# A small store of zeros ahead of ScalarE's loads, in a kernel that scales an image by channel

## The chip, the cores and the metric

The kernel runs on one core of a Trainium2 chip. The metric is the device time of one execution in microseconds (us). Before the change the median of the three runs was 530.68 us (530.67 to 531.29).

## The reference

```python
# x: [1, 384, 384, 384] bf16 (113.25 MB), w1d: [1] bf16
g = einsum("bhwc->bc", x) / (H * W)      # mean of each channel
s = sigmoid(g * w1d[0])                  # k = 1: one weight
return x * s[:, None, None, :]           # another 113.25 MB
```

The input must be read once and the output written once, 226.5 MB together. A strict reading needs the mean of all of x before the first element can be written. The kernel gets round this: it computes a scale `s_early` from the first tile alone, multiplies everything with it, sums up the whole of x on TensorE along the way, computes the true scale `s_true` at the end, and repeats the work only if the two differ after rounding to bf16. They don't with this input.

## The kernel before: the parts that matter

The image is cut into 27 tiles, 25 of them of 128 partitions x 44 rows x 384 channels (4.33 MB) and two smaller ones at the end. Six of them fit into SBUF at once. The first four are loaded in halves, one half from SyncE's queue and one from ScalarE's; all further loads come from SyncE and all stores from ScalarE.

```python
def load(place, n, r0, queues=("sync",)):
    ...
    for queue, m in zip(queues, split(n, -(-n // len(queues)))):
        plan.dma(queue, at(place + i, m), of[:, i * C : (i + m) * C],
                 writes=rows(place + i, m))
        i += m

def put(place, n, r0, to):
    plan.op("vector", gate(to, place, n, s_early), ...)      # x * s_early
    plan.final.append(
        plan.dma("scalar", dram(o_rows, r0, n), at(to, n), reads=rows(to, n)))

# cut: add_rows (TensorE sums a tile), add_banks, weight
plan.op("vector", lambda e: e.memset(ones[:], 1.0), writes=["ones"])
for k in range(BOTH):                                        # BOTH = 4
    load(places[k], sizes[k], starts[k], ("sync", "scalar"))
    if k == 0:
        plan.dma("scalar", w_one[0:1, 0:1], w1d.unsqueeze(0), writes=["w_one"])
weight()
add_rows(places[0], sizes[0], 0, True, True)
add_banks(0, copy=True)
# cut: s_early = sigmoid(total * w), on ScalarE
for k in range(1, len(sizes)):
    if k >= n_slots:                                         # n_slots = 6
        j = k - n_slots
        put(places[j], sizes[j], starts[j], places[j])       # store tile k - 6
    if k >= BOTH:
        load(places[k], sizes[k], starts[k])                 # waits for that store
    add_rows(places[k], sizes[k], 1, k == 1, k == last)
# cut: the last stores, s_true, the comparison, the second pass
```

Of the kernel before, what the change touches and what calls it, by code (L numbers as in the profile page):

```python
# [3 lines left out]
P = 128  # L4
ROW = 384
BF16 = mybir.dt.bfloat16
# [99 lines left out]
def split(n, most):  # L106
    k = -(-n // most)
    return [n // k + (i < n % k) for i in range(k)]
# [6 lines left out]
def bass_standalone__channel_attn_eca__vision_kernel(  # L115
# [5 lines left out]
    B, H, W, C = x.shape  # L121
    assert B == 1 and C == ROW and (B * H * W) % (4 * P) == 0
    n_rows = B * H * W // P
    x_rows, o_rows = x.flatten_outer_dims(), out.flatten_outer_dims()

    def dram(view, r0, n):
        return view[r0 * P : (r0 + n) * P, :].rearrange("(p t) c -> p (t c)", p=P)
# [3 lines left out]
    s_true = nc.alloc_sbuf_tensor("s_true", [P, C], BF16)  # L131
    w_one = nc.alloc_sbuf_tensor("w_one", [1, 16], BF16)
    w_scaled = nc.alloc_sbuf_tensor("w_scaled", [P, 2], F32)
    warm = nc.alloc_sbuf_tensor("warm", [P, 2], F32)
    wrong = nc.alloc_sbuf_tensor("wrong", [P, 1], F32)
    redo = nc.alloc_sbuf_tensor("redo", [P, 1], I32)
# [9 lines left out]
    def at(r0, n):  # L146
        assert r0 + n <= n_arena
        return arena[:, r0 * C : (r0 + n) * C]

    def rows(r0, n):  # L150
        return [("sb", r) for r in range(r0, r0 + n)]

    def gate(to, place, n, s):
        s_b = s[:].unsqueeze(1).broadcast_to([P, n, C])
        v, to_v = (at(r, n).rearrange("p (t c) -> p t c", t=n) for r in (place, to))
        return lambda e: e.tensor_tensor(to_v, v, s_b, ALU.mult)  # L156
# [5 lines left out]
    sizes = [EDGE] + [SLOT] * full + [4 * q for q in split(rest // 4, EDGE // 4)]  # L162
    assert sum(sizes) == n_rows and max(sizes) <= SLOT
    plan = Planner(nc, "a", 50)
# [51 lines left out]
    def add_banks(group, copy):  # L216

        for m, lo, hi in ((0, 0, C), (0, C, WIDE), (1, 0, 256), (1, 256, WIDE),
# [9 lines left out]
                )  # L228
            plan.op("vector", emit, reads=[f"acc{group}", "total"], writes=["total"])

    def put(place, n, r0, to):
        plan.op(
            "vector",
            gate(to, place, n, s_early),
            reads=["s_early"] + rows(place, n),
            writes=rows(to, n),
        )
        plan.final.append(
            plan.dma("scalar", dram(o_rows, r0, n), at(to, n), reads=rows(to, n))
        )  # L240

    def weight():
# [28 lines left out]


    plan.op("gpsimd", lambda e: e.memset(warm[:, 0:1], 0.0), writes=["warm"])  # L273
    plan.op("vector", lambda e: e.memset(ones[:], 1.0), writes=["ones"])  # L274
    for k in range(BOTH):
        load(places[k], sizes[k], starts[k], ("sync", "scalar"))
# [10 lines left out]
        reads=["total", "w_scaled0", "warm1"],  # L287
        writes=["s_early"],
# [4 lines left out]
    for k in range(1, len(sizes)):  # L293
        if k >= n_slots:
            j = k - n_slots
            put(places[j], sizes[j], starts[j], places[j])
        if k >= BOTH:
            load(places[k], sizes[k], starts[k])
        add_rows(places[k], sizes[k], 1, k == 1, k == last)
    for k in range(len(sizes) - n_slots, last):  # L300
        put(places[k], sizes[k], starts[k], places[k])
    put(places[last], sizes[last], starts[last], places[last + 1 - n_slots])


# [6 lines left out]
        reads=["total", "w_scaled1"],  # L311
        writes=["s_true"],
# [6 lines left out]
        reads=["s_true", "s_early"],  # L319
        writes=["total"],  # L320
# [4 lines left out]
        reads=["total"],  # L325
        writes=["wrong"],
# [4 lines left out]
        reads=["wrong"],  # L331
        writes=["redo"],
# [5 lines left out]
    for place, n, r0 in zip(places, sizes, starts):  # L338
# [4 lines left out]
            reads=rows(place, n),  # L343
            writes=rows(place, n),
# [74 lines left out]
```

## Time and profile before

| | before |
|---|---|
| time, median of 3 runs | 530.68 us |
| span in the profile | 528.7 us |
| TensorE and VectorE busy | 46% each |
| DMA, mean over the span | 429 GB/s |

These lines are from the page of the kernel before. "DMA" is the busy share of the core's 16 DMA engines in tenths, in 40 equal slices of the span; "GB/s" is what they moved in each slice. The last two lines are DMA issues: the queue that issues them (ACTq is ScalarE's, SPq SyncE's), the KB of each and the median time in us from issue to landing.

```profile
span 528.7 us, 1091 instructions
...
DMA  8999999999999999999999999999999999999998
GB/s 359 431 427 419 447 429 431 445 414 447 419 442 437 422 447 412 450 428 430 440 419 450 430 429 435 424 450 430 430 431 427 447 429 430 429 443 433 430 420 349
...
HBM read 113.25 MB, written 113.25 MB: 428 GB/s over the span
...
out_dram<-arena ACTq DMA_DIRECT2D x25, 4224.0 KB, 62.3
arena<-in_x_dram SPq DMA_DIRECT2D x21, 4224.0 KB, 38.7
```

The DMA engines are full from the second slice to the last but one, and no compute engine comes close. The windows say the same with numbers (a packet is counted whole in the window in which it starts, so a share can pass 1). Columns: the window in us from the start of the span, its length, busy time of each engine with the count of instructions, TensorE's granted clock, the share of the DMA engines' time, and GB/s in the last column. Kernel before:

```profile
core 0: us, PE busy (x) PEld busy (x) DVE busy (x) ACT busy (x) POOL busy (x), PEclk, DMA share, GB/s
0.00:5.00 5.00, 0.00 (x0) 0.00 (x0) 0.17 (x1) 1.49 (x2) 0.30 (x5) 1.00 0.68 237
...
35.00:60.00 25.00, 15.57 (x65) 0.00 (x0) 24.28 (x4) 0.00 (x0) 0.00 (x0) 0.91 1.02 433
60.00:110.00 50.00, 24.77 (x79) 0.00 (x0) 20.86 (x3) 0.00 (x0) 0.00 (x0) 0.64 1.00 432
110.00:500.00 390.00, 184.59 (x646) 0.00 (x0) 179.61 (x21) 0.00 (x0) 0.00 (x0) 0.73 1.00 433
```

The next lines are from the timeline of the beginning, kernel before: start in us, duration in us, engine, line, operation, tiles; what stands in brackets at the end is the idle time just ahead and what ended it. A DMA's duration here is the time its queue took to issue it, not the transfer.

```profile
0.73 0.41 ACTq L91 DMA_DIRECT2D arena<-in_x_dram  x1
...
0.74 2.96 SPq L91 DMA_DIRECT2D arena<-in_x_dram  x6
...
1.17 0.54 ACTq L91 DMA_DIRECT2D w_one<-in_w1d_dram  x1
1.74 1.59 ACTq L91 DMA_DIRECT2D arena<-in_x_dram  x3
...
14.13 0.16 PE L252 MATMUL w_all<-w_one,ones 1*128 1x1 bf16 x1 [14.13 <-DMA w_one<-in_w1d_dram]
...
25.92 0.61 ACT L284 ACTIVATE s_early<-total,w_scaled 128x384 bf16<-128x384 f32 x1 [21.06 <-DVE total L226]
...
35.56 18.07 ACTq L91 DMA_DIRECT2D out_dram<-arena  x3
```

By 3.7 us, SyncE has issued six loads and ScalarE four. TensorE's first matmul waits for the weight, which stands in ScalarE's queue behind a half tile and is there at 14.1 us. `s_early` is made at 25.9 us and the first store is issued at 35.6 us. From then on the kernel has one rhythm, which the chain of waits shows (start, duration, what; "another core or an unknown queue" here is the time of a DMA that the profile doesn't name). Kernel before:

```profile
44.43 41.95 DMA out_dram<-arena
...
86.45 0.33 SPq L91
86.78 19.55 another core or an unknown queue
...
106.39 0.33 SPq L91
```

SyncE issues a load every 19.9 us, each time when a store has landed and freed its place. A tile loaded and a tile stored are 8.65 MB, and 8.65 MB in 19.9 us is about 433 GB/s again: the rhythm is set by the DMA engines' rate.

The trace also has a record of every DMA packet; the packet figures in this document are worked out from these records, and none of the views printed here shows them. Here one packet is one partition's piece, 16,896 bytes for a half tile and 33,792 for a whole one. A large piece takes 1.251 us on its engine, and 16 engines at that pace make 432.2 GB/s. "Lost", below, is the time by which the DMAs are behind that rate. In the kernel before they lose 2.56 us first (the first packet starts only at 1.75 us, and the first ones are slow), about 0.4 us around 44 us, where the first store begins, and 2.2 us at the end, where the engines don't finish together and the last packet ends at 527.8 us, 0.9 us before the span does.

### The profile page before, as it was taken

Reading aid. Unit: us, or ns where it says so; the run is one execution under the profiler, and the core shown is the slowest. Engines: PE = TensorE matmul, PEld = TensorE weight load, DVE = VectorE, ACT = ScalarE, POOL = GpSimd, SP = SyncE. Lnnn points to the kernel's source line nnn. Section 1 sums busy time; section 2 is a strip of 40 time slices with the busy share of each in tenths; the row PEclk is TensorE's granted clock in tenths of the full one; section 3 lists DMA queues with packets and bytes.
Section 4 is the critical chain, followed back from the end, with each engine's and each line's share of the span. In section 5 each row is a group of like instructions: output and inputs, shape, how many; then the busy total and the mean of one; then the engine's idle time right before and its main releaser. Section 6 shows DMA issues by size and latency. Waiting matters only on the chain.

```text
span 528.7 us, 1091 instructions
## 1 busy us (share of the span) xinstructions
PE 245.2 (46%) x865; PEld 0.2 (0%) x2; DVE 241.2 (46%) x45; ACT 2.7 (1%) x4; POOL 0.3 (0%) x5
## 2 busy tenths in 40 slices
PE   0877256165275165174274364264373373365400
PEld 0000000000000000000000000000000000000000
DVE  0299742633624633624624624624615615616720
ACT  1000000000000000000000000000000000000000
POOL 0000000000000000000000000000000000000000
PEclk9989776686676786786875786886875776877665
DMA  8999999999999999999999999999999999999998
GB/s 359 431 427 419 447 429 431 445 414 447 419 442 437 422 447 412 450 428 430 440 419 450 430 429 435 424 450 430 430 431 427 447 429 430 429 443 433 430 420 349
DMA packets 8360, 226.57 MB, mean 429 GB/s; under 512 B 930, under 2 KB 930, under 8 KB 930
## 3 DMA queue, kind: packets, MB, share of 16 engines
q10 hardware_dynamic: 4466, 121.90, 53.5%
q1 hardware_dynamic: 3888, 104.60, 46.1%
q8 instruction: 3, 0.05, 0.0%
q14 instruction: 3, 0.02, 0.0%
HBM read 113.25 MB, written 113.25 MB: 428 GB/s over the span
## 4 chain that ended last, share of the span: by engine, by line
another core or an unknown queue 70%; DMA 16%; DVE 4%; PE 3%; SPq 1%; issue 1%; ACT 0%; ACTq 0%
DMA out_dram<-arena 8%; DMA arena<-in_x_dram 6%; PE acc L184 3%; DVE arena L156 3%; DMA w_one<-in_w1d_dram 2%; SPq L91 1%; DVE total L226 1%; ACT s_true L308 0%; ACT s_early L284 0%; DVE total L316 0%; DVE total L224 0%; DVE wrong L324 0%; PE acc L182 0%; ACTq L91 0%
## 5 line engine op out<-in xcount | busy, mean ns | idle before, releaser
L184 PE MATMUL acc<-arena,ones 128*128 128x512 bf16 x863 | 244.7, 454 | 244.0 <-DMA arena<-in_x_dram 244.0
L156 DVE TENSOR_TENSOR arena<-arena,s_early 128x16896 bf16<-128x16896 bf16 (+2 forms) x27 | 234.5, 8691 | 240.9 <-PE acc L184 237.5
L252 PE MATMUL w_all<-w_one,ones 1*128 1x1 bf16 x1 | 0.2, 159 | 14.1 <-DMA w_one<-in_w1d_dram 14.1
L261 DVE TENSOR_SCALAR w_scaled<-w_all 128x1 f32<-128x1 f32 x2 | 0.2, 152 | 13.3 <-PE w_all L252 13.3
L226 DVE TENSOR_TENSOR total<-total,acc 128x128 f32<-128x128 f32 (+2 forms) x11 | 4.5, 408 | 2.4 <-PE acc L184 2.0
L224 DVE COPY total<-acc 128x384 f32<-128x384 f32 x1 | 0.6, 558 | 8.6 <-PE acc L184 8.6
L308 ACT ACTIVATE s_true<-total,w_scaled 128x384 bf16<-128x384 f32 x1 | 0.6, 614 | 479.5 <-DVE total L226 479.5
L246 ACT ACT_TABLE_LOAD x1 | 1.3, 1283 | 3.4 <-issue 3.4
L316 DVE TENSOR_TENSOR total<-s_true,s_early 128x384 f32<-128x384 uint16 x1 | 0.6, 559 | 0.7 <-ACT s_true L308 0.7
L284 ACT ACTIVATE s_early<-total,w_scaled 128x384 bf16<-128x384 f32 x1 | 0.6, 614 | 21.1 <-DVE total L226 21.1
L182 PE MATMUL acc<-arena,ones 128*128 128x512 bf16 x1 | 0.6, 590 | 0.0
L324 DVE TENSOR_REDUCE wrong<-total 128x1 f32<-128x384 f32 x1 | 0.6, 553 | 0.0
L274 DVE MEMSET ones<- 128x128 bf16 x1 | 0.2, 165 | 0.8 <-PEq L404 0.8
L246 ACT ACTIVATE warm<-warm 128x1 f32<-128x1 f32 x1 | 0.2, 203 | 0.0
L330 DVE CAST redo<-wrong 128x1 int32<-128x1 f32 x1 | 0.2, 154 | 0.0
L182 PEld LDWEIGHTS acc<-arena,ones 128*128 128x128 bf16 x1 | 0.1, 105 | 0.0
L252 PEld LDWEIGHTS w_all<-w_one,ones 1*128 1x128 bf16 x1 | 0.1, 99 | 14.1 <-issue 14.1
L404 POOL MEMSET const-bfloat16-1.0<- 128x1 bf16 x1 | 0.1, 102 | 0.0
L404 POOL MEMSET const-uint8-127<- 128x1 uint8 x1 | 0.1, 102 | 0.0
L273 POOL MEMSET warm<- 128x1 f32 x1 | 0.1, 99 | 0.3 <-POOLq L404 0.3
L404 POOL MEMSET const-float32-0.0<- 128x1 f32 x1 | 0.1, 99 | 0.2 <-issue 0.2
L404 POOL MEMSET const-float32-1.0<- 128x1 f32 x1 | 0.1, 99 | 0.0
## 6 DMA issues: line engine op xcount, KB each, us to landing
out_dram<-arena ACTq DMA_DIRECT2D x25, 4224.0 KB, 62.3
arena<-in_x_dram SPq DMA_DIRECT2D x21, 4224.0 KB, 38.7
arena<-in_x_dram ACTq DMA_DIRECT2D x4, 2112.0 KB, 27.2
arena<-in_x_dram SPq DMA_DIRECT2D x4, 2112.0 KB, 26.9
arena<-in_x_dram SPq DMA_DIRECT2D x1, 2688.0 KB, 35.1
out_dram<-arena ACTq DMA_DIRECT2D x1, 2688.0 KB, 29.2
arena<-in_x_dram SPq DMA_DIRECT2D x1, 2304.0 KB
out_dram<-arena ACTq DMA_DIRECT2D x1, 2304.0 KB, 26.9
```

Source lines behind the costliest of these rows:

```text
L91: ("op", lambda e: e.dma_start(out, in_), self.pool[i], 16)
L156: return lambda e: e.tensor_tensor(to_v, v, s_b, ALU.mult)
L182: loaded.append(e.matmul(bank, weights, moving, start=start, stop=stop))
L184: return e.add_instruction(mybir.InstMatmult(name=nc.get_next_instruction_name(), engine=mybir.EngineType.PE, ins=[e.lower_ap(moving), e.l ...
L224: emit = lambda e, part=part, of=of: e.tensor_copy(part, of)
L226: emit = lambda e, part=part, of=of: e.tensor_tensor(part, part, of, ALU.add)
L246: lambda e: e.activation(warm[:, 1:2], warm[:, 0:1], ACT_F.Sigmoid),
L284: lambda e: e.activation(s_early[:], total[:], ACT_F.Sigmoid, scale=w_scaled[:, 0:1]),
L308: lambda e: e.activation(s_true[:], total[:], ACT_F.Sigmoid, scale=w_scaled[:, 1:2]),
L316: lambda e: e.tensor_tensor(total[:], s_true[:].bitcast(U16), s_early[:].bitcast(U16), ALU.not_equal),
L324: lambda e: e.reduce_max(wrong[:], total[:], axis=mybir.AxisListType.X),
L404: nc = _bacc.Bacc("TRN2", target_bir_lowering=False, num_devices=1)
```

## The change

Ahead of everything else in ScalarE's queue comes a store of zeros into 16 rows of the first tile of the output, 768 bytes each. The tile's own store overwrites them later, so the result is the same. The intent, as far as the code shows it, is to pay some cost of a first write early, where it may hide.

```diff
+    zeros = nc.alloc_sbuf_tensor("zeros", [P, C], BF16)
...
+    def touch():
+        plan.op("vector", lambda e: e.memset(zeros[:], 0.0), writes=["zeros"])
+        plan.dma(
+            "scalar", dram(o_rows, 0, sizes[0])[0:P:8, 0:C], zeros[0:P:8, :],
+            reads=["zeros"], writes=["touched"],
+        )
...  # in put():
-            plan.dma("scalar", dram(o_rows, r0, n), at(to, n), reads=rows(to, n))
+            plan.dma("scalar", dram(o_rows, r0, n), at(to, n),
+                     reads=rows(to, n) + ["touched"])
...
     plan.op("gpsimd", lambda e: e.memset(warm[:, 0:1], 0.0), writes=["warm"])
+    touch()
     plan.op("vector", lambda e: e.memset(ones[:], 1.0), writes=["ones"])
```

More of the change, by code (lines that the diff above doesn't have):

```diff
@@ L238, in put @@
         plan.final.append(
-            plan.dma("scalar", dram(o_rows, r0, n), at(to, n), reads=rows(to, n))
+            plan.dma(
+                "scalar",
+                dram(o_rows, r0, n),
+                at(to, n),
+                reads=rows(to, n) + ["touched"],
+            )
         )
```

## The prediction

> **What bounds the kernel now.** The DMA engines, almost everywhere. 226.57 MB move at 429 GB/s over a span of 528.7 us. Windows of 5 us between 35 and 130 us show 429 to 433 GB/s. PE and DVE are 46% busy. The chain of waits repeats a period of 19.9 us per tile: 8.65 MB in 19.9 us is again some 433 GB/s. The Trainium skill, page "DMA: Bandwidth & Descriptors", section "Issuing engines are not separate DMA queues", says that DMAs from all engines interleave on the same 16 DMA engines; the trace agrees: both queues together hold 433 GB/s.
>
> **Where DMA time is lost.** In the packet records a 33,792-byte packet takes 1.251 us, which is 432 GB/s on 16 engines. Against that rate the DMAs lose
> - 1.75 us before the first packet, and 0.8 us more by 5 us: the first load packets take 1.07 to 1.57 us, later ones of that size 0.63;
> - 0.39 us between 42 and 46 us, where the first store begins: the load packet just ahead of an engine's first store packet takes 1.3 to 2.3 us instead of 1.25. This looks like a one-time cost of the first write; later stores show none;
> - about 2.1 us at the end: engines finish between 525.9 and 527.8 us.
>
> All of it is under 1%; what the change can address, 0.39 us, is 0.07%.
>
> **What the change adds.** A DVE memset of 128x192 words (estimate 0.2 us: the 128x128 one takes 0.165); one ScalarE DMA issue (0.36 to 0.65 us by that queue's records) waiting for it; 12 KB, presumably one packet per engine; a wait before the first store that is long over at 35.6 us; tiles shifted by 768 bytes in SBUF. Nothing is removed; all else keeps its order on each engine.
>
> **What moves.** ScalarE's first half load is issued about 0.8 us later (0.73 to about 1.5 us). SyncE's loads fill the engines meanwhile: six are issued by 3.7 us, and ScalarE's packets began only at 2.85 us anyway. The weight, queued behind that half (landed at 14.0 us), and s_early (25.9 us) may come up to 1 us later. That costs nothing: the first store, issued at 35.6 us, stands behind the half loads until about 43 us, some 7 us of slack. A one-time first-write cost moves from 43 us to about 3 us, where it is partly hidden beside the slow first loads or just paid there.
>
> **Predicted.** Gain 0 to 0.4 us if the first write's cost is hidden, loss 0 to 0.5 us if it stalls the starting loads longer; skew of the engines at the end adds some tenths either way. I expect 530.5 us, 8 in 10 between 529.8 and 531.4. Faster by over 2%: 1%; within 2%: 98%; slower by over 2%: 1%.
>
> **What would show it.** Right: ScalarE's first half load issued near 1.5 us; steady windows at 433 GB/s and the period of 19.9 us unchanged; 42 to 46 us without its loss of 0.39 us, which is found, wholly or in part, in the first 5 us. Wrong: the loss at 43 us stays (then it belongs to the switch from loads to loads with stores); or the first 5 us lose over 1 us more.
>
> **What would make it wrong.** A tiny store that stalls its engines for microseconds, or an order of the two queues that changes the steady rate or the skew at the end (now 1.9 us).

## The result and the profile after

Throughout, a ratio is the mean time of one kernel's runs over the mean of the other's of the same rounds, so it isn't quite the ratio of the medians quoted beside it. Executions over 1.5% slower than the fastest of the same kernel are left out of the means.

| | before | after |
|---|---|---|
| median | 530.65 us (530.33 to 531.29, 6 runs) | 531.02 us (530.72 to 531.37, 6 runs) |
| ratio | | 1.0007, 95% interval 0.9994 to 1.002 |
| span of the profiled run | 528.7 us | 529.6 us |

The times are the same within what the runs can tell. The page after:

```profile
span 529.6 us, 1094 instructions
...
GB/s 362 430 440 402 444 424 427 421 442 434 424 444 426 436 436 424 443 424 436 436 426 444 426 431 439 426 442 429 429 440 426 436 436 424 435 432 439 424 432 341
...
HBM read 113.25 MB, written 113.26 MB: 428 GB/s over the span
```

The windows after:

```profile
core 0: us, PE busy (x) PEld busy (x) DVE busy (x) ACT busy (x) POOL busy (x), PEclk, DMA share, GB/s
0.00:5.00 5.00, 0.00 (x0) 0.00 (x0) 0.36 (x2) 0.63 (x1) 0.30 (x5) 1.00 0.70 247
...
35.00:60.00 25.00, 14.62 (x53) 0.00 (x0) 23.56 (x3) 0.00 (x0) 0.00 (x0) 0.80 1.03 431
60.00:110.00 50.00, 29.70 (x117) 0.00 (x0) 28.35 (x4) 0.00 (x0) 0.00 (x0) 0.80 1.01 429
110.00:500.00 390.00, 182.73 (x633) 0.00 (x0) 181.87 (x27) 0.00 (x0) 0.00 (x0) 0.73 1.00 433
```

The steady part, 110 to 500 us, is at 433 GB/s as before, and so is the rhythm in the chain of waits after:

```profile
49.72 42.10 DMA out_dram<-arena
...
91.88 0.33 SPq L91
92.21 19.61 another core or an unknown queue
...
111.89 0.33 SPq L91
```

It stands 5.4 us later (91.88 us where before had 86.45), but its period is still 19.9 to 20.0 us. The beginning is what changed. Timeline after:

```profile
0.73 3.13 SPq L91 DMA_DIRECT2D arena<-in_x_dram  x6
0.84 0.22 DVE L237 MEMSET zeros<- 128x192 uint32 x1 [0.84 <-PEq L422]
...
1.09 0.61 ACTq L91 DMA_DIRECT2D out_dram<-zeros  x1
1.74 0.60 ACTq L91 DMA_DIRECT2D arena<-in_x_dram  x1
...
18.14 0.16 PE L269 MATMUL w_all<-w_one,ones 1*128 1x1 bf16 x1 [18.14 <-DMA w_one<-in_w1d_dram]
...
31.22 0.61 ACT L302 ACTIVATE s_early<-total,w_scaled 128x384 bf16<-128x384 f32 x1 [25.35 <-DVE total L227]
...
40.85 18.08 ACTq L91 DMA_DIRECT2D out_dram<-arena  x3
```

ScalarE's first half load is issued at 1.74 us instead of 0.73, the weight is used at 18.14 us instead of 14.13, `s_early` is made 5.3 us later and the first store is issued 5.3 us later. Everything that depends on ScalarE's queue is late by 4.0 to 5.4 us, and the time barely moves.

The packet records add what the windows can't show. Loss against 432.2 GB/s, in us:

| lost in us | before | after |
|---|---|---|
| first 8 us | 2.56 | 2.58 |
| 8 to 120 us | 0.50 | 1.14 |
| 120 to 520 us | -0.56 | -0.62 |
| 520 us to the end of the span | 2.2 | 2.4 |

The 16 small pieces begin between 5.5 and 6.2 us and take 0.036 us each. They cost nothing in the first 8 us. The slow packets ahead of the first store, 0.36 us per engine in before, have not gone: they moved along with the store, from 42 to 44 us to 50 to 52 us, and are 0.51 us in this profile. In addition there is a second place of that kind near 87 us, 0.49 us, around the end of the second store and the beginning of the third. That one is not in the profile of before.

### The profile page after: what moved, and what is told of

Same layout as the page of the kernel before. It is cut to its first block, busy times and chain, and to the rows that moved or that the text cites. A ratio compares the mean times of both kernels' runs of the same rounds, so it can differ in the third digit from the quotient of the medians.

```text
span 529.6 us, 1094 instructions
## 1 busy us (share of the span) xinstructions
PE 243.9 (46%) x865; PEld 0.2 (0%) x2; DVE 241.3 (46%) x46; ACT 2.7 (1%) x4; POOL 0.3 (0%) x5
## 4 chain that ended last, share of the span: by engine, by line
another core or an unknown queue 70%; DMA 15%; DVE 4%; PE 3%; issue 1%; SPq 1%; ACT 0%; ACTq 0%
DMA out_dram<-arena 8%; DMA arena<-in_x_dram 4%; DMA w_one<-in_w1d_dram 3%; PE acc L185 3%; DVE arena L157 2%; SPq L91 1%; DVE total L227 1%; ACTq L91 0%; ACT s_true L326 0%; ACT s_early L302 0%; DVE total L334 0%; DVE total L225 0%; DVE wrong L342 0%; PE acc L183 0%
```

## The experiments

Twelve runs were made, each with its own expectation. All gave correct results. The table puts their main readings side by side. "Large packets" is when the first large packet of ScalarE's queue begins. "Ahead of store" is the extra time of slow packets within 2.6 us of the first store packet, mean per engine; "second stall" is the largest such sum elsewhere up to 130 us, within 4 us (values under 0.1 are put as none).

| kernel | median us | ratio to before (95%) | large packets | first store issued | ahead of store | second stall |
|---|---|---|---|---|---|---|
| before | 530.65 | | 2.85 | 35.56 | 0.36 | none |
| after | 531.02 | 1.0007 (0.9994 to 1.002) | 6.78 | 40.85 | 0.51 | 0.49 |
| e1, before again | 530.63 | 0.9996 (0.9982 to 1.001) | 2.97 | 37.07 | 0.31 | none |
| e2, after again | 530.92 | 1.0004 (0.9991 to 1.0018) | 6.83 | 40.65 | 0.28 | 0.69 |
| e3, memset alone | 530.49 | 0.9994 (0.998 to 1.0007) | 2.91 | 36.20 | 0.64 | none |
| e4, wait alone | 530.86 | 1.0005 (0.9991 to 1.0019) | 5.39 | 38.49 | 0.47 | none |
| e5, small load | 530.93 | 1.0003 (0.999 to 1.0016) | 6.68 | 39.84 | 0.61 | none |
| e6, 128 pieces | 531.18 | 1.0008 (0.9996 to 1.0021) | 10.77 | 43.68 | 0.40 | none |
| e7, later in the queue | 530.82 | 1.0003 (0.999 to 1.0015) | 2.88 | 38.18 | 0.51 | none |
| e8, 40 memsets | 531.12 | 1.0015 (1.0 to 1.003) | 18.34 | 55.62 | 0.34 | none |
| e9, 120 memsets | 543.24 | 1.0241 (1.0223 to 1.0259) | 42.58 | 73.67 | 0.02 | see text |
| e10, last tile | 530.92 | 1.0009 (0.9996 to 1.0022) | 6.78 | 40.43 | 0.50 | none |
| e12, small load again | 530.96 | 1.002 (1.0004 to 1.0036) | 6.69 | 40.56 | 0.53 | none |

e11 is told in its own paragraph. Some expectations quote sums of slow packets that differ a little from this table (0.44 or 0.64 us, for instance).

Theory A says that the DMA engines' rate and the bytes set the time, that the queues hold enough loads for ScalarE's start not to matter, and that the loss ahead of the first store belongs to that store. Its rival B says that the small store does take a first-write cost away, and that a new cost of equal size hides it.

### e1: the kernel before, as its own control

No edit.

> The kernel before, unchanged, as its own control. Both theories (A: the DMA engines are the limit and a few tenths lost at the start of a store just move; B: the touch removes a first-write loss of 0.39 us and another loss of the same size cancels it): ratio 1.000 within 0.001. Its profile tells how repeatable the small losses are: A and B both expect the load packets ahead of the first store packets to take 1.3 to 2.3 us near 42 us again, about 0.4 us per engine, and no second stall of that kind. If a second stall shows up here too, the one at 87 us in the changed kernel's profile is chance.

530.63 us against 530.76, ratio 0.9996. The slow packets ahead of the first store were there again (0.31 us), and no second stall. The first store was issued at 37.07 us in this profile against 35.56 in the other, so 1.5 us of movement there is chance.

### e2: the kernel after, once more

No edit.

> The changed kernel, unchanged, for a second profile. A: ratio 1.000 to 1.001; the stall ahead of the first store (near 50 us, 0.44 us per engine) is there again, since the touch does not remove it. If the stall near 87 us (0.49 us per engine) belongs to the change, it is there again; if it was chance, it is gone and the span is some 0.5 us shorter than 529.6. B: the first-store stall would have to be absent.

530.92 us, ratio 1.0004. The loss ahead of the first store was there (0.28 us) and so was the second stall (0.69 us). B needed the first of these to be absent. So B falls in this form, and the second stall is no accident of one profile.

### e3: the zeros and their memset, without the store

```diff
-        plan.dma("scalar", dram(o_rows, 0, sizes[0])[0:P:8, 0:C], zeros[0:P:8, :],
-                 reads=["zeros"], writes=["touched"])
 # cut: put() loses its + ["touched"], as in e4, e5 and e12
```

> The tensor of zeros and its memset alone, no store and no wait on ScalarE's queue: tiles shifted by 768 bytes and 0.2 us of VectorE work. A: as the kernel before, ratio 0.999 to 1.001; ScalarE's first load packets start near 2.85 us and the first store is issued near 35.6 us. If the placement of the tiles were what moves the second queue back, they would start near 5 us or later, as in the changed kernel.

530.49 us, ratio 0.9994; ScalarE's large packets at 2.91 us and the first store at 36.20 us. The shift of the tiles by 768 bytes and the memset do nothing that shows beside the control.

### e4: the wait alone

```diff
 # on top of e3, in load()
+                reads=["zeros"] if r0 == 0 and queue == "scalar" else [],
```

> As e3, but ScalarE's first half load waits for the memset of zeros, so it is issued near 1.09 us instead of 0.73; no small store. Two theories of why ScalarE's packets begin at 6.8 us in the changed kernel instead of 2.85: G (arriving behind SyncE's second and third load where descriptors are made is what costs) expects first ScalarE packets at 4.5 us or later here too, and the first store near 39 to 41 us; C (the small store itself is slow) expects them near 3.2 to 3.7 us and the first store near 36 us. Time: ratio 0.999 to 1.001 under both.

Timeline of e4:

```profile
1.09 0.40 ACTq L91 DMA_DIRECT2D arena<-in_x_dram  x1
...
38.49 18.07 ACTq L91 DMA_DIRECT2D out_dram<-arena  x3
```

The half load is issued 0.36 us later than in before, and its packets begin 2.54 us later (5.39 instead of 2.85 us). There is no small store here. So 2.54 of the 3.93 us by which ScalarE's large packets are late in after come with the later issue alone, and theory C, which expected 3.2 to 3.7 us, falls. The other 1.39 us come with the small DMA ahead of them, which also puts off the issue of the half load from 1.09 to 1.74 us, and e5 shows the same with a load. The first store was issued at 38.49 us, between what C (36 us) and G (39 to 41 us) expected. The part of G that names a place, behind SyncE's second and third load where descriptors are made, is not shown by this; e8 speaks against it. The time is that of before, ratio 1.0005.

### e5 and e12: a small load in place of the small store

```diff
-            "scalar", dram(o_rows, 0, sizes[0])[0:P:8, 0:C], zeros[0:P:8, :],
-            reads=["zeros"], writes=["touched"],
+            "scalar", zeros[0:P:8, :], dram(x_rows, 0, sizes[0])[0:P:8, 0:C],
+            writes=["zeros"],
```

> The small store replaced by a load of the same 16 pieces of 768 bytes at the same place in ScalarE's queue, with the same wait. If the stall near 87 us (0.49 and 0.64 us per engine in two profiles of the changed kernel, absent in the profiles of before, of its control, of the memset alone and of the wait alone) comes from an additional small transfer in the queue, whatever its direction, it is here too; if it comes from the early write to the output, it is absent and only the stall ahead of the first store is left. ScalarE's first large packets near 6.8 us, as with the small store, under both. Ratio 0.999 to 1.001.

> The small load of e5 again, for a second profile and a closer time. If the stall near 87 us needs the early write, it is absent again; if it comes by chance of how the queues stand, it may show. The ratio is 0.999 to 1.001.

Ratios 1.0003 and 1.002; two of e12's six runs were at 531.82 and 533.72 us, and they make its ratio, which lies outside the 0.999 to 1.001 that was expected, and its wide interval. ScalarE's queue begins at 6.68 and 6.69 us, as with the store: for the beginning it makes no difference whether the 16 pieces are written or read. The loss ahead of the first store stays, 0.61 and 0.53 us. The second stall was absent from both profiles. (The small load was issued at 1.09 us, like the small store.)

### e6: all 128 rows of the tile

```diff
-            "scalar", dram(o_rows, 0, sizes[0])[0:P:8, 0:C], zeros[0:P:8, :],
+            "scalar", dram(o_rows, 0, sizes[0])[:, 0:C], zeros[:, :],
```

> The small store with all 128 rows of the tile, 128 pieces of 768 bytes instead of 16. If the loss ahead of the first store were a first write to cold places of the output and 16 pieces were too few to take it away, it is gone here (under 0.05 us per engine between 45 and 60 us). If it belongs to the beginning of a large store beside a load, it stays at 0.25 to 0.6 us. Time: ratio 0.999 to 1.0015 either way.

531.18 us, ratio 1.0008. By about 10.5 us 768 bytes had been written in each of the first tile's 128 pieces, one per partition, and the loss ahead of the first store was still 0.40 us. So it is not a cost that an earlier write of 768 bytes in each piece takes away. A write of the whole tile ahead was not tried. But the later stores of before, each to places that this execution had not written yet, show no such loss up to 120 us. The second stall was absent, though this kernel writes the same rows early too.

### e7: the small store behind the first half load

```diff
-    touch()                                # ahead of everything
...
         if k == 0:
+            touch()                        # between the half load and the weight
             plan.dma("scalar", w_one[0:1, 0:1], w1d.unsqueeze(0), writes=["w_one"])
```

> The small store moved behind ScalarE's first half load. Theory G (what delays ScalarE's queue is being issued behind SyncE's second and third load) expects the first half load at 2.9 us again, as before, and the first store issued at 35.5 to 37.5 us; the small pieces come behind those 8 packets per engine, near 13 us. The stall ahead of the first store stays. If the time of the changed kernel differed from before by the late start of ScalarE's queue, this one is as fast as before; the difference is at most 0.4 us, so this may not show. Ratio 0.999 to 1.001.

530.82 us, ratio 1.0003. The large packets of ScalarE's queue begin at 2.88 us, as before. The first store was issued at 38.18 us, 0.7 us later than the range that was expected. The time does not tell it from after or before.

### e8: ScalarE's queue 13 us later

```diff
-        plan.op("vector", lambda e: e.memset(zeros[:], 0.0), writes=["zeros"])
+        for _ in range(40):
+            plan.op("vector", lambda e: e.memset(zeros[:], 0.0), writes=["zeros"])
```

> The changed kernel with 40 memsets of zeros instead of one, so that ScalarE's queue begins some 10 us later. Theory A (the queues hold enough loads; when ScalarE's queue starts is off the critical path) expects the first store to be issued 8 to 14 us later than in the changed kernel (49 to 55 us) and no idle DMA: 5 us windows at 420 GB/s or more up to 100 us, and a time within 0.5 us of the changed kernel's. If the late start were what costs the changed kernel its few tenths, this one is slower by 1 us or more.

Timeline of e8, then its windows:

```profile
0.84 12.89 DVE L238 MEMSET zeros<- 128x192 uint32 x40 [0.84 <-PEq L423]
...
13.77 0.61 ACTq L91 DMA_DIRECT2D out_dram<-zeros  x1
...
55.62 0.36 ACTq L91 DMA_DIRECT2D out_dram<-arena  x1
```

```profile
core 0: us, PE busy (x) PEld busy (x) DVE busy (x) ACT busy (x) POOL busy (x), PEclk, DMA share, GB/s
35.00:60.00 25.00, 18.50 (x67) 0.00 (x0) 13.84 (x8) 0.61 (x1) 0.00 (x0) 0.86 1.01 431
60.00:110.00 50.00, 36.68 (x159) 0.00 (x0) 43.24 (x6) 0.00 (x0) 0.00 (x0) 0.86 1.01 431
```

ScalarE's queue begins at 13.77 us and the first store is issued at 55.62 us, 0.6 us beyond the expected range, 15 us later than in after and 20 us later than in before. The two long windows are at the rate of before. In windows of 5 us from 15 to 100 us the DMA lies between 409 and 449 GB/s; two of them, at 418 and 409, are under the 420 that was expected, with no idle stretch. The median is 531.12 us, 0.1 us above that of after. Three of its six runs were at 530.7 us, and one at 533.41 us gave the mean its 1.0015. So a delay of 13 us costs at most some tenths, where a delay that counted fully would have cost 13.

This run also bears on where ScalarE's queue is held up. SyncE's last load of the beginning had been issued by 3.8 us, and the small store still took 3.9 us from its issue at 13.77 us to its first packet at 17.67. Hence the wait needs no load that is being issued at that moment; busy DMA engines are enough. That agrees with each engine having taken some packets of the other queue ahead, but no run shows that directly.

### e9: ScalarE's queue 39 us later

The same edit with 120 memsets.

> 120 memsets of zeros instead of 40, so that ScalarE's queue begins near 40 us; this is to find where its slack ends. Theory A, worked out from the traces of before and of e8: SyncE's six loads (17.3 MB) are drained near 42 us, ScalarE's four half loads (8.65 MB) near 62 us, but the first tile is only whole near 48 us, and from there to the first store e8 took 22.5 us (33.1 to 55.6), so that the first store is issued near 70 us. The DMA is then idle for 7 to 9.5 us between 62 and 72 us, and the time is 7 to 10 us over before: ratio 1.013 to 1.019. The rival, that the start of ScalarE's queue costs in proportion (e8 cost at most 0.5 us for 13 us), expects under 2 us, ratio under 1.004.

Timeline of e9, then its windows:

```profile
73.67 0.36 ACTq L91 DMA_DIRECT2D out_dram<-arena  x1
```

```profile
core 0: us, PE busy (x) PEld busy (x) DVE busy (x) ACT busy (x) POOL busy (x), PEclk, DMA share, GB/s
50.00:62.00 12.00, 10.67 (x38) 0.10 (x1) 0.67 (x2) 0.00 (x0) 0.00 (x0) 1.00 1.00 429
62.00:64.00 2.00, 2.00 (x11) 0.00 (x0) 1.86 (x5) 0.00 (x0) 0.00 (x0) 1.00 0.73 313
64.00:66.00 2.00, 1.95 (x10) 0.00 (x0) 1.33 (x1) 0.61 (x1) 0.00 (x0) 1.00 0.06 25
66.00:74.00 8.00, 8.00 (x39) 0.00 (x0) 8.00 (x2) 0.00 (x0) 0.00 (x0) 1.00 0.00 0
74.00:80.00 6.00, 5.95 (x28) 0.00 (x0) 6.00 (x1) 0.00 (x0) 0.00 (x0) 1.00 1.05 451
```

543.24 us, ratio 1.0241, 12.7 us over before: the rival, which expected under 2 us, falls. Here the queues ran dry: from about 64 to 74 us the DMA engines stand still, until the first store is issued at 73.67 us. The packet records put the loss between 60 and 80 us at 10.9 us. The kind of loss was as A expected and its size was not (7 to 10 us): the first tile was whole at 51.2 us instead of 48, and every step after that moved along. Its second half began at 42.6 us only, and one of the 16 engines delivered its share 1.4 us after the other fifteen (51.2 against 49.8 us).

The limit can be estimated, and e8 and e9 lie on either side of it. Six tiles of loads, 25.95 MB, are issued without waiting for any store; at 432.2 GB/s they last 60.0 us, and with the 2.56 us lost at the beginning the DMA has work until about 62.6 us; in e9 it ran dry between 62 and 64 us. A first store issued before that (35.6, 40.9 and 55.6 us) costs some tenths at most; one at 73.7 us costs what the engines stand idle. Where between 55.6 and 73.7 us the cost sets in was not measured.

The loss just ahead of the first store is absent here (0.02 us), where no load ran beside it. But slow packets stood elsewhere. From 42.6 to 48.1 us ScalarE's first half load lost 0.45 us per engine, beside the small store and SyncE's last loads, when no large store had begun; from 85 to 92 us and from 101 to 105 us there were slow packets again, about 1.0 us and 0.5 us per engine. With the 10.9 us these come to 12.9 us, close to the 12.7 us by which the run is longer.

### e10: the small store into the last tile's rows

```diff
-            "scalar", dram(o_rows, 0, sizes[0])[0:P:8, 0:C], zeros[0:P:8, :],
+            "scalar", dram(o_rows, starts[last], sizes[last])[0:P:8, 0:C], zeros[0:P:8, :],
```

> The small store put into the last tile's rows of the output instead of the first's. If the stall near 87 us (in both profiles of the changed kernel, 0.4 to 0.64 us per engine; absent in all others) comes from having written the first tile's rows early, it is absent here; if any early write brings it, it is here; if it is a matter of how the two queues happen to stand to each other, either may come. The stall ahead of the first store (near 50 us) stays. Ratio 0.999 to 1.0015.

530.92 us, ratio 1.0009. The loss ahead of the first store was 0.50 us, the same as with the first tile's rows. The second stall was absent. Together with e6, which writes the first tile early and has no second stall, this leaves neither "any early write" nor "an early write to the first tile" as its cause by itself.

### e11: the small store in SyncE's queue

```diff
-            "scalar", dram(o_rows, 0, sizes[0])[0:P:8, 0:C], zeros[0:P:8, :],
+            "sync", dram(o_rows, 0, sizes[0])[0:P:8, 0:C], zeros[0:P:8, :],
```

> The small store at the head of SyncE's queue instead of ScalarE's, so that ScalarE's half load is issued first. Theory G (the queue that is issued some 0.35 us after the other comes behind that one's next loads) expects the mirror image: ScalarE's large packets begin near 1.75 us, SyncE's only at 4.5 us or later. As ScalarE's half of the first tile then comes early but SyncE's late, the first store is again issued later than 35.6 us (38 to 42 us), and the time is the same: ratio 0.999 to 1.0015.

Three of its seven runs were slow, the profiled one (539.2 us) among them, and one took 577.36 us; the same rounds of before had none. The four fast runs give 1.0003 (0.9989 to 1.0018). Why this kernel had slow runs is not known, and nothing is built on them. The one reading taken from the profile is the order of the beginning: ScalarE's packets start at 1.74 us, SyncE's small pieces at 5.41 and its large ones at 6.7 us, the mirror image of the kernel after (1.75, 5.49 and 6.78). The queue that comes second is the one held up, whichever it is.

## Why the prediction was right, and where it was not

**The time.** 530.5 us was predicted with 529.8 to 531.4; 531.02 was measured, within 2%, as predicted. What carried it was the first reading: DMA engines at 433 GB/s for the whole of the span, and a change that adds 12 KB to 226.5 MB. e8 shows that ScalarE's queue can begin 13 us later for some tenths of a us at most, and e9 shows that 39 us are too many.

**"A one-time first-write cost moves from 43 us to about 3 us."** This step failed. In both profiles of after the loss stayed ahead of the first store (0.51 and 0.28 us) and moved with it to 50 us. It remained when 768 bytes of every piece had been written before (e6) and when the small transfer was a load (e5, e12). The small store itself cost nothing in the first 8 us (2.58 us lost there against 2.56). The prediction had named this outcome as its "wrong" branch and the switch from loads alone to loads with stores as the reason in that case. That fits the loss ahead of the first store in all profiles, among them e9, where the first store met no loads and the loss ahead of it was absent; but no run takes the switch apart further, and it can't be the whole account of slow packets: e9 lost as much (0.45 us) near 43 us before any large store, and the second stall stands at no first store. So the gain that the change could have brought was not there to be had. The check that "42 to 46 us" would be without its loss came out as predicted and proved nothing, because the store had left that stretch.

**"May come up to 1 us later."** This step had the size wrong. The weight came 4.0 us later and `s_early` 5.3 us. The mis-sized term is the hold-up of ScalarE's queue: 0.8 us was reckoned for the later issue alone. e4 shows that 0.36 us at the issue already becomes 2.5 us at the first packet. The conclusion "that costs nothing" held to within some tenths of a us, although the delay of `s_early` was five times what was reckoned; that it held is owed to slack that the prediction had not counted, for the 7 us that it rested on were a wrong measure as well. They were counted to 43 us, when the first store could have begun behind the half loads; the limit that counts is the end of the issued loads, near 62.6 us.

**The sign.** A gain of 0.2 us was expected and a loss of 0.4 us was measured. The interval includes no change, so this is not settled. What can be said: e1 and e3, which leave ScalarE's queue as it was, came out at 0.9996 and 0.9994, and all kernels that hold up a queue's beginning or put something into it came out between 1.0003 and 1.002, leaving out e9. Nearly every one of these has an interval that includes 1. The raw runs lean towards a small loss: the eleven of after have a mean of 531.04 us, the fifteen of before in the same rounds 530.72 us, and all five of e6 (531.09 to 531.37 us) lie above all eleven of before in its rounds (530.38 to 530.95 us). Where the tenths go differs from profile to profile. The profiles of after lost 0.6 us more than before between 8 and 120 us, and the second stall accounts for most of it. Those of e4 and e8 have no second stall and spans just as long (529.6 and 529.7 us); they lost 2.9 us after 520 us, where before lost 2.2. And both profiled runs (531.37 and 531.30 us) are among the slower of their kernel: seven of its eleven runs lie between 530.72 and 531.07 us, four between 531.30 and 531.53. Whether the second stall is what separates these groups is not shown.

**Open.** What the packets wait for ahead of the first store and near 43 us in e9, what brings the second stall (in the two profiles of after, and something like it in e9, but in no other fast one), and what holds up the second queue at the beginning.

## What to carry to other kernels

When the DMA engines are full and the queues hold loads issued in advance, a delay at the head of one queue can cost next to nothing (some tenths of a us here, for 13 us) as long as the issued work lasts; work out that moment from the bytes issued and the measured rate, and compare it with the first transfer that must refill the queue. A small loss seen at the first transfer of a kind is not yet a first-use cost: do the small transfer early and see whether the loss stays where it was, moves with the large one, or goes. And check that a hoped-for gain is larger than the spread between runs before building on it: the whole of this one was 0.07% of the time.

## What the Trainium skill lacked or had wrong

- "DMA: Bandwidth & Descriptors", section "Latency and other measured facts", gives about 600 ns to the first byte of a DMA that SyncE or ScalarE issues. With idle engines the trace of after agrees: SyncE's first issue ended at 1.12 us and its first packet began at 1.75 us, 0.63 us later. It has no figure for the wait of a DMA that comes to engines busy with the other queue: there the small store's first packet began 3.3 us after the end of its issue in e8 (14.38 to 17.67 us) and 3.8 us after it in after (1.70 to 5.49 us).
- The same page, section "Where 436 GB/s comes from", says that for transfers between HBM and SBUF the HBM side, about 358 GB/s, binds. Here one core held 433 GB/s for 390 us with loads and stores mixed. The page "HBM Reference", section "Specifications (TRN2)", has about 425 GB/s for a core that streams alone, which these runs agree with far better.
- No page tells of the loss at the first large store that begins beside a running load: 0.28 to 0.64 us per engine in all fast profiles here but that of e9, where no load ran beside it.
